# A dense GELU layer, forward and backward, on one core: half products of two step pairs in one run, output units by twos

## The chip, the cores and the metric

The kernel runs on one core of a Trainium2 chip. The time is the device time of one execution in microseconds (us), the median of several runs; less is better. A profiled execution stands beside it: its trace names every instruction of every engine with its start and length.

## What is computed

One layer with a GELU between two matrix products, its output, and the gradients of all five inputs. All tensors are bf16; x and grad_out are 2048 x 448, w1 is 448 x 1792, w2 is 1792 x 448.

```python
def _fwd_reference(x, w1, b1, w2, b2):
    h = jnp.einsum("bsd,df->bsf", x, w1) + b1
    h = _gelu(h)                       # tanh approximation
    return jnp.einsum("bsf,fd->bsd", h, w2) + b2

def reference(x, w1, b1, w2, b2, grad_out):
    ...
    _out, _vjp = jax.vjp(_f, x, w1, b1, w2, b2)
    _grads = _vjp(grad_out)
    return (_out0, *[jnp.asarray(_g) for _g in _grads])
```

In words: u = x w1 + b1, h = gelu(u), out = h w2 + b2; q = grad_out w2', gh = gelu'(u) q, grad_x = gh w1', and the gradients of w1, b1, w2 and b2 from x, gh, h and grad_out.

## The kernel before

The 2048 rows are cut into four blocks of 512, the 1792 hidden columns into fourteen tiles of 128. A step g (0 to 27) is one block with a pair of hidden tiles; there are seven steps in a block. Everything in a step is kept transposed: 128 hidden columns on the partitions, 512 rows along the free axis, two tiles side by side.

A step's work on TensorE:

- **M1** (L242, matmuls at L250) multiplies u's three full slices of 128 of the 448 inner columns, for both tiles: six matmuls of 512 columns.
- **rest** (L253) is what is left of 448: 64 rows. u's half (L260) sits in rows 64 to 127 of the array, q's half (L263) in rows 0 to 63, so that one of each can run beside the other. A call of rest issues u's halves of step g + 1 in turn with q's halves of step g. A pair of such matmuls is called a slot below, and the halves of one call a run.
- **M4** (L266, L269) adds q's three full slices: six matmuls.
- **products** (L432): 448-column matmuls that multiply a finished h or gh tile into out or grad_x. A Unit (L414) is 128 rows of out ("o") or grad_x ("g") and needs fourteen products; 32 units make 448 products.

ScalarE's part (L290): two copies of u out of PSUM with the bias (L294), the square (L295), the GELU (L296), and after VectorE's cubic term the tanh (L390). VectorE's part: the cubic term into B (dve_first, L387), the slope p (L394), two small steps and a product (L395 to L397), and the gate (L401), which reads q from PSUM and writes gh. V, A and B have one buffer each, so that ScalarE's copy for a step waits for VectorE's cubic term of the step before, and its square for p of the step before.

PSUM has eight banks of 512 f32 columns per partition. Before: two for u (one tile), two for q (one tile), four ("acc", L65) that go round for the units. Each unit is evicted by itself (L440): grad_x and the first two units of block 0 by ScalarE (L446), the other out units by VectorE with b2 added (L448). Two units share a staging tile and one store, issued by GpSimd (L452).

The order is written out by hand (manual schedule); each engine works through its own instructions in program order and waits where data or a buffer is not there. The loop (L501) does, per step: rest, M4, evictions, gate, ScalarE's and VectorE's first half for step g + 1, the second half, then products, then M1 of step g + 2. In block 0 the products of its own four out units are run as h comes up (grow, L474): eight a step. From step 7 on there are twelve products a step, in block 3 sixteen. GpSimd's queue also stores h to DRAM (L405), for the turned loads later; SP's queue turns gh into natural order (L410) and loads the next blocks of x and grad_out (L149, L167).

After the steps, GpSimd reloads x and grad_out in natural order over the places of w1 and w2' (L549, L550), eight units of block 3 are left on TensorE, and SP loads h turned (L562). Then come the gradients of w1 (L598, L606) and of w2 (L617), whose results go round the same four banks. VectorE and GpSimd sum the gradients of the biases beside them.

Of the kernel before, what the change touches and what calls it, by code (L numbers as in the profile page):

```python
# [18 lines left out]
def kernel(  # L19
# [44 lines left out]
    psum_u = ctx.enter_context(tc.tile_pool(name="psum_u", bufs=1, space=bass.MemoryType.PSUM))  # L64
    psum_a = ctx.enter_context(tc.tile_pool(name="psum_a", bufs=4, space=bass.MemoryType.PSUM))  # L65

    first = ExitStack()
    psum_h = first.enter_context(tc.tile_pool(name="psum_h", bufs=1, space=bass.MemoryType.PSUM))

# [172 lines left out]
    def M1(g):  # L242
        if g == 0:
            u_of[g] = [psum_a.tile([P, SB], F32, name="acc")[:] for h in range(2)]
        else:
            u = psum_u.tile([P, 2, SB], F32, name="u")
            u_of[g] = [u[:, h, :] for h in range(2)]
        for h in range(2):
            for kt in range(KF):
                nc.tensor.matmul(u_of[g][h], lhsT=w1_sb[:, 1 + kt, cols(g, h)], rhs=xq(g // NPAIR)[:, 1 + kt, :],  # L250
                                 start=(kt == 0), stop=False, skip_group_check=True)

    def rest(gu, gg):  # L253

        if gg is not None:
            q = psum_g.tile([P, 2, SB], F32, name="q")
            g_of[gg] = q
        for h in range(2):
            if gu is not None:
                nc.tensor.matmul(u_of[gu][h], lhsT=w1_sb[DL:P, 0, cols(gu, h)], rhs=xq(gu // NPAIR)[DL:P, 0, :],  # L260
                                 start=False, stop=True, tile_position=(DL, 0), skip_group_check=True)
            if gg is not None:
# [23 lines left out]
    def keep_warm(n, weights, moving):  # L286
        for i in range(n):
            nc.tensor.matmul(pw[:], lhsT=weights, rhs=moving, start=True, stop=True)

    def act_first(g):  # L290
# [4 lines left out]
        nc.scalar.activation(out=A_of(g), in_=V_of(g), func=ACT.Square, scale=math.sqrt(3.0 * GELU_C * GELU_A))  # L295
        nc.scalar.activation(out=hT(g), in_=V_of(g), func=ACT.Gelu_apprx_tanh)  # L296

    def first_products():

        u_of[0] = [[t[:, 0:HB] for t in ua], [psum_h.tile([P, SB], F32, name="h%d" % h)[:, 0:HB] for h in range(2)]]  # L300
# [12 lines left out]
    def turn_w2():  # L313

        for kt in range(KD):
            n = DL if kt == KF else P
            for h in range(2):
                o = (2 * (kt % 2) + h) * P
                nc.tensor.matmul((ta, pw)[kt // 2][0:n, o:o + P], lhsT=w2_sb[:, h, kt * P:kt * P + n], rhs=ident,
                                 start=True, stop=True)  # L320

    def turned(i):
        nc.scalar.copy(out=w2T_sb[:, 2 * i:2 * i + 2, 0:2 * P], in_=(ta, pw)[i].rearrange("p (k f) -> p k f", k=2))

    def first_chain():
# [52 lines left out]
        for r in range(2):  # L378
            first_q(r, (0, 1))
            run_pieces([U["o", 0, r]] * 2)  # L380
# [10 lines left out]


    def dve_second(g):
        nc.vector.scalar_tensor_tensor(out=p_of(g), in0=A_of(g), scalar=GELU_C, in1=hT(g), op0=ALU.add, op1=ALU.mult)  # L394
        nc.vector.tensor_scalar(out=t_of(g), in0=t_of(g), scalar1=1.0, scalar2=None, op0=ALU.add)  # L395
        nc.vector.tensor_scalar(out=p_of(g), in0=p_of(g), scalar1=-0.5, scalar2=None, op0=ALU.add)  # L396
        nc.vector.tensor_tensor(out=t_of(g), in0=t_of(g), in1=p_of(g), op=ALU.mult)  # L397

# [15 lines left out]
    class Unit:  # L414
        def __init__(self, kind, b, j):
            self.kind, self.b, self.j, self.done, self.ps = kind, b, j, 0, None

            self.by_act = kind == "g" or (b == 0 and j < 2)

        def piece(self):  # L420
            ft = self.done
            c, h = divmod(ft, 2)
            g = self.b * NPAIR + c
            if self.ps is None:
                self.ps = psum_a.tile([P, SB], F32, name="acc")
            js = slice(self.j * P, (self.j + 1) * P)
            if self.kind == "o":
                lhsT, rhs = hT(g)[:, h, js], w2_sb[:, ft, :]
            else:
                lhsT, rhs = ghT(g)[:, h, js], w1T_sb[:, ft, :]  # L430
            bias = self.by_act and self.kind == "o"
            nc.tensor.matmul(self.ps[:, 0:D], lhsT=lhsT, rhs=rhs, start=(ft == 0), stop=(ft == NF - 1 and not bias))  # L432
            if bias and ft == NF - 1:
                nc.tensor.matmul(self.ps[:, 0:D], lhsT=w128[:], rhs=b2_bc[:], start=False, stop=True)
            self.done += 1
            return self.done == NF

    stage = {}

    def evict(un):  # L440
        key = (un.kind, un.b, un.j // 2)
        if key not in stage:
            stage[key] = iop.tile([P, 2, D], BF16, name="io_" + un.kind)
        st = stage[key]
        if un.by_act:
            nc.scalar.copy(out=st[:, un.j % 2, :], in_=un.ps[:, 0:D])  # L446
        else:
            nc.vector.tensor_tensor(out=st[:, un.j % 2, :], in0=un.ps[:, 0:D], in1=b2_bc[:], op=ALU.add)  # L448
        dst = out2 if un.kind == "o" else gx2
        if un.j % 2:  # L450
            r0 = row0(un.b) + (un.j - 1) * P
            nc.gpsimd.dma_start(out=dst[r0:r0 + 2 * P, :].rearrange("(j p) d -> p j d", p=P), in_=st[:])  # L452

    full = []

    def run_pieces(units):
        for un in units:
            if un.piece():
                full.append(un)

    def flush(by_act=None):
        for un in [un for un in full if by_act in (None, un.by_act)]:
            full.remove(un)
# [193 lines left out]
```

## Time and profile before

| | us |
|---|---|
| median of 3 runs | 275.22 (275.17 to 275.58) |
| the profiled execution, its own time | 274.79 |
| span of its trace (first to last instruction) | 273.0 |
| TensorE busy in the span | 267.8 |
| VectorE busy | 193.1 |
| ScalarE busy | 145.0 |
| steps of block 0: ended on TensorE at about | 47 |
| gradient of w1 begins (L598) | 184.40 |
| gradient of w2 begins (L617) | 227.3 |

TensorE is called PE in the rows, its weight loads PEld, VectorE DVE, ScalarE ACT, GpSimd POOL and SyncE SP; L432 is line 432 of the kernel. A row names the tile that is written, an arrow and the tiles that are read, and "x12" is twelve instructions. Matmuls overlap: a row's length is that of one matmul from its first to its last work, so the spacing of the starts, and not the lengths, says what TensorE needs. The page's chain is the sequence of work that ended last, followed back from the end; what is not in it had time to spare.

### The profile page before, as it was taken

How to read it: one execution, taken by the hardware profiler on the slowest of the kernel's cores; microseconds unless marked ns; L12 is line 12 of the kernel's file. 1: busy time of each engine (PE TensorE's matmuls, PEld its weight loads, DVE VectorE, ACT ScalarE, POOL GpSimd, SP SyncE). 2: the span in 40 equal slices, each digit the busy share in tenths (PEclk: the TensorE clock that was granted, in tenths of full speed). 3: DMA queues.
4: the chain of work that ended last, by engine and by line, in shares of the span. 5: the costliest groups of instructions: out<-in, count | busy, mean ns of one | idle time of the engine just before them, and what ended most of it. 6: DMA issues, size and time to landing. Idle time of an engine off the chain costs nothing.

```text
span 273.0 us, 3631 instructions
## 1 busy us (share of the span) xinstructions
PE 267.8 (98%) x1411; PEld 124.9 (46%) x1411; DVE 193.1 (71%) x242; ACT 145.0 (53%) x193; POOL 54.2 (20%) x59
## 2 busy tenths in 40 slices
PE   8999999999999999999999999999999999999995
PEld 3434443444444344434444445554445655555552
DVE  6899999999999999999888861139999980000000
ACT  3988879788888788877777740011111221112111
POOL 0000103820401403023022137111700019400000
PEclk9999999999999999999999999999999999999999
DMA  7999899999279928065534239999999951101110
GB/s 172 209 272 227 155 211 187 260 285 242 74 167 223 235 57 170 17 170 131 116 113 87 100 113 223 257 331 251 188 245 259 184 143 58 52 2 50 53 50 34
DMA packets 100477, 43.52 MB, mean 159 GB/s; under 512 B 89036, under 2 KB 97100, under 8 KB 100460
## 3 DMA queue, kind: packets, MB, share of 16 engines
q1 hardware_dynamic: 93376, 26.65, 51.2%
q0 software_dynamic: 4512, 14.69, 17.0%
q10 hardware_dynamic: 2572, 1.95, 2.4%
q8 instruction: 11, 0.18, 0.3%
q14 instruction: 6, 0.05, 0.1%
HBM read 7.00 MB, written 14.23 MB: 78 GB/s over the span
## 4 chain that ended last, share of the span: by engine, by line
PE 84%; DVE 12%; DMA 2%; ACT 0%; issue 0%; DVEq 0%
PE acc L432 27%; PE acc L617 16%; PE acc L598 13%; PE q L269 10%; PE u L250 10%; PE u L260 4%; DVE T L394 3%; DVE Bt L387 3%; DVE ghT_h L401 3%; PE acc L606 2%; DVE T L397 2%; DMA xg_h<-in_x_dram 2%; DVE T L395 1%; PE h L282 1%; DVE T L396 1%; PE acc L305 0%
## 5 line engine op out<-in xcount | busy, mean ns | idle before, releaser
L432 PE MATMUL acc<-w_gw,hT_h 128*128 128x448 bf16 x224 | 46.6, 353 | 0.0
L432 PE MATMUL acc<-w1T_gw,ghT_h 128*128 128x448 bf16 x224 | 45.1, 352 | 0.0
L294 ACT ACTIVATE VA<-u,b_col 128x512 f32<-128x512 f32 x54 | 34.0, 681 | 13.4 <-PE u L260 13.4
L250 PE MATMUL u<-xg_h,w_x 128*128 128x512 bf16 x162 | 39.4, 379 | 0.6 <-ACT VA L294 0.6
L269 PE MATMUL q<-xg_h,w2T_g 128*128 128x512 bf16 x162 | 39.6, 381 | 0.0
L401 DVE SCALAR_TENSOR_TENSOR ghT_h<-T,q 128x1024 bf16<-128x1024 bf16 x27 | 32.9, 1220 | 8.0 <-PE q L269 6.6
L598 PE MATMUL acc<-gh_nat,w_x 128*128 128x512 bf16 (+1 forms) x192 | 36.7, 353 | 0.0
L390 ACT ACTIVATE T<-Bt 128x1024 bf16<-128x1024 f32 x27 | 28.5, 1057 | 13.2 <-DVE Bt L387 13.1
L394 DVE SCALAR_TENSOR_TENSOR T<-VA,hT_h 128x1024 bf16<-128x1024 f32 x27 | 33.1, 1226 | 0.0
L387 DVE SCALAR_TENSOR_TENSOR Bt<-VA 128x1024 f32<-128x1024 f32 x27 | 32.9, 1218 | 0.0
L432 PEld LDWEIGHTS <-hT_h 128*128 128x128 bf16 x224 | 21.8, 98 | 21.2 <-issue 0.2
L432 PEld LDWEIGHTS <-ghT_h 128*128 128x128 bf16 x224 | 21.9, 98 | 20.9
L583 DVE TENSOR_TENSOR VA<-VA,gh_nat 128x1792 f32<-128x1792 f32 x14 | 30.0, 2142 | 0.5
L295 ACT ACTIVATE VA<-VA 128x1024 f32<-128x1024 f32 x27 | 28.5, 1057 | 0.9
L296 ACT ACTIVATE hT_h<-VA 128x1024 bf16<-128x1024 f32 x27 | 28.1, 1040 | 0.0
L598 PEld LDWEIGHTS <-w_x 128*128 128x128 bf16 x192 | 18.7, 98 | 17.7 <-issue 0.4
L269 PEld LDWEIGHTS <-w2T_g 128*128 128x128 bf16 x162 | 13.6, 97 | 24.2 <-issue 11.4
L619 ACT CAST w_gw<-acc 128x448 bf16<-128x448 f32 x13 | 6.9, 533 | 32.6 <-PE acc L617 32.6
L250 PEld LDWEIGHTS <-w_x 128*128 128x128 bf16 x162 | 15.8, 98 | 18.4 <-issue 0.8
L600 ACT CAST w1T_gw<-acc 128x512 bf16<-128x512 f32 (+1 forms) x12 | 6.3, 533 | 30.1 <-PE acc L598 23.0
L446 ACT CAST io_g<-acc 128x448 bf16<-128x448 f32 x16 | 8.3, 520 | 22.6 <-PE acc L432 22.6
L405 POOL DMA_DIRECT2D hT_dram<-hT_h x28 | 20.3, 727 | 0.2 <-issue 0.2
(79 smaller groups left out, 245.4 us busy)
## 6 DMA issues: line engine op xcount, KB each, us to landing
hT_dram<-hT_h POOLq DMA_DIRECT2D x28, 256.0 KB, 4.0
out_dram<-io_o POOLq DMA_DIRECT2D x8, 224.0 KB, 3.8
out_dram<-io_g POOLq DMA_DIRECT2D x8, 224.0 KB, 3.2
w_x<-in_x_dram POOLq DMA_DIRECT2D x1, 1344.0 KB, 11.9
w2T_g<-in_grad_out_dram POOLq DMA_DIRECT2D x1, 1344.0 KB, 15.2
out_dram<-w_gw SPq DMA_DIRECT2D x4, 336.0 KB, 2.4
w_x<-in_w_dram SPq DMA_DIRECT2D x2, 384.0 KB, 4.2
out_dram<-w1T_gw ACTq DMA_DIRECT2D x2, 384.0 KB, 4.0
```

Of the source, the lines that this page charges most:

```text
L250: nc.tensor.matmul(u_of[g][h], lhsT=w1_sb[:, 1 + kt, cols(g, h)], rhs=xq(g // NPAIR)[:, 1 + kt, :], start=(kt == 0), stop=False, skip_grou ...
L269: nc.tensor.matmul(g_of[g][:, h, :], lhsT=w2T_sb[:, kt, cols(g, h)], rhs=gq(g // NPAIR)[:, kt, :], start=False, stop=(kt == KF - 1), skip_ ...
L294: nc.scalar.activation(out=V_of(g)[:, h, :], in_=u[h], func=ACT.Identity, bias=b1_col[:, ft:ft + 1])
L295: nc.scalar.activation(out=A_of(g), in_=V_of(g), func=ACT.Square, scale=math.sqrt(3.0 * GELU_C * GELU_A))
L387: nc.vector.scalar_tensor_tensor(out=B_of(g), in0=A_of(g), scalar=3.0 * GELU_C, in1=V_of(g), op0=ALU.add, op1=ALU.mult)
L390: nc.scalar.activation(out=t_of(g), in_=B_of(g), func=ACT.Tanh, scale=-1.0 / 3.0)
L394: nc.vector.scalar_tensor_tensor(out=p_of(g), in0=A_of(g), scalar=GELU_C, in1=hT(g), op0=ALU.add, op1=ALU.mult)
L401: nc.vector.scalar_tensor_tensor(out=ghT(g), in0=t_of(g), scalar=1.0, in1=q[:], op0=ALU.add, op1=ALU.mult)
L432: nc.tensor.matmul(self.ps[:, 0:D], lhsT=lhsT, rhs=rhs, start=(ft == 0), stop=(ft == NF - 1 and not bias))
L583: nc.vector.tensor_tensor(out=gsb_v, in0=gsb_v, in1=gh_rows(st, 0, NF), op=ALU.add)
L598: nc.tensor.matmul(psv, lhsT=x_all[:, st, kt * P:(kt + 1) * P], rhs=gh_rows(st, a0, a1), start=(st == 0), stop=(st == NS - 1))
L617: nc.tensor.matmul(ps[:, 0:D], lhsT=h_blk[ft][:, st, :], rhs=g_all[:, st, :], start=(st == 0), stop=(st == NS - 1))
```

## The change

PSUM is dealt out anew: four tiles of two banks each, named x, y, z and w. x and y hold u, z and w hold q; the units use them in between. In block 0 the order of the first six steps is as before, with y and w holding the four growing out units.

From step 7 on, the loop goes once for step 7 and then by two steps, a and a + 1. One call of rest issues the halves of u for two steps and of q for two steps: four slots in one run. Then come M4(a) and M4(a + 1), three matmuls of M1, two whole units (28 products) that are run in z, once the gate of step a has read q out of it, and the other nine matmuls of M1. The two units are evicted by one instruction of 2 x 448 elements, before ScalarE's and VectorE's second half for the later step. For the lone step 7 the units go to w. In steps 26 and 27 there is no u left, so q's halves run by themselves.

At the end of block 0, step 7's chain is taken apart: the two evictions of block 0's out units stand between its square and its GELU on ScalarE, and between p and the small steps on VectorE, and M1 of steps 8 and 9 follow at once. out(3, 0) and (3, 1) are run in the double step 24, before the last M4; three pairs of units are left for after the steps. Loads of the next blocks, stores of h and the turning of gh are placed at other steps. The gradients' results go round x, y, w, z, the first bank of each.

The core of the diff, from which lines that only leave are left out in the loop and the unit code (they stand in the kernel above):

```diff
@@ -61,11 +61,16 @@
     const = ctx.enter_context(tc.tile_pool(name="const", bufs=1))
     iop = ctx.enter_context(tc.tile_pool(name="iop", bufs=2))
     dram = ctx.enter_context(tc.tile_pool(name="dram", bufs=1, space=bass.MemoryType.DRAM))
-    psum_u = ctx.enter_context(tc.tile_pool(name="psum_u", bufs=1, space=bass.MemoryType.PSUM))
-    psum_a = ctx.enter_context(tc.tile_pool(name="psum_a", bufs=4, space=bass.MemoryType.PSUM))
-
+
+
+
+    psum_s = ctx.enter_context(tc.tile_pool(name="psum_s", bufs=1, space=bass.MemoryType.PSUM))
     first = ExitStack()
     psum_h = first.enter_context(tc.tile_pool(name="psum_h", bufs=1, space=bass.MemoryType.PSUM))
+
+    def pair(name):
+        return (psum_z if name == "z" else psum_s).tile([P, 2, SB], F32, name=name)
+
 
     hT_dram = dram.tile([F, S], BF16, name="hT_dram")
     hT_dram_v = hT_dram.rearrange("(ft p) s -> p ft s", p=P)
@@ -239,27 +244,25 @@
     u_of = {}
     g_of = {}
 
-    def M1(g):
-        if g == 0:
-            u_of[g] = [psum_a.tile([P, SB], F32, name="acc")[:] for h in range(2)]
-        else:
-            u = psum_u.tile([P, 2, SB], F32, name="u")
-            u_of[g] = [u[:, h, :] for h in range(2)]
-        for h in range(2):
+    def M1(g, u, hs=(0, 1)):
+        u_of[g] = [u[:, h, :] for h in range(2)]
+        for h in hs:
             for kt in range(KF):
                 nc.tensor.matmul(u_of[g][h], lhsT=w1_sb[:, 1 + kt, cols(g, h)], rhs=xq(g // NPAIR)[:, 1 + kt, :],
                                  start=(kt == 0), stop=False, skip_group_check=True)
 
-    def rest(gu, gg):
-
-        if gg is not None:
-            q = psum_g.tile([P, 2, SB], F32, name="q")
+    def rest(us, qs):
+
+        for gg, q in qs:
             g_of[gg] = q
-        for h in range(2):
-            if gu is not None:
+        for i in range(2 * max(len(us), len(qs))):
+            n, h = divmod(i, 2)
+            if n < len(us):
+                gu = us[n]
                 nc.tensor.matmul(u_of[gu][h], lhsT=w1_sb[DL:P, 0, cols(gu, h)], rhs=xq(gu // NPAIR)[DL:P, 0, :],
                                  start=False, stop=True, tile_position=(DL, 0), skip_group_check=True)
-            if gg is not None:
+            if n < len(qs):
+                gg, q = qs[n]
                 nc.tensor.matmul(q[:, h, :], lhsT=w2T_sb[0:DL, KF, cols(gg, h)], rhs=gq(gg // NPAIR)[0:DL, KF, :],
                                  start=True, stop=False, tile_position=(0, 0), skip_group_check=True)
 
...
-    def act_first(g):
+            nc.tensor.matmul(tp[:, 1, :], lhsT=weights, rhs=moving, start=True, stop=True)
+
+    def act_copy(g):
         u = u_of.pop(g)
         for h in range(2):
             ft = 2 * (g % NPAIR) + h
             nc.scalar.activation(out=V_of(g)[:, h, :], in_=u[h], func=ACT.Identity, bias=b1_col[:, ft:ft + 1])
         nc.scalar.activation(out=A_of(g), in_=V_of(g), func=ACT.Square, scale=math.sqrt(3.0 * GELU_C * GELU_A))
+
+    def act_gelu(g):
         nc.scalar.activation(out=hT(g), in_=V_of(g), func=ACT.Gelu_apprx_tanh)
 
+    def act_first(g):
+        act_copy(g)
+        act_gelu(g)
+
...
-    def dve_second(g):
+    def dve_p(g):
         nc.vector.scalar_tensor_tensor(out=p_of(g), in0=A_of(g), scalar=GELU_C, in1=hT(g), op0=ALU.add, op1=ALU.mult)
+
+
+    def dve_rest(g):
         nc.vector.tensor_scalar(out=t_of(g), in0=t_of(g), scalar1=1.0, scalar2=None, op0=ALU.add)
         nc.vector.tensor_scalar(out=p_of(g), in0=p_of(g), scalar1=-0.5, scalar2=None, op0=ALU.add)
         nc.vector.tensor_tensor(out=t_of(g), in0=t_of(g), in1=p_of(g), op=ALU.mult)
+
+    def dve_second(g):
+        dve_p(g)
+        dve_rest(g)
 
...
-    class Unit:
-        def __init__(self, kind, b, j):
-            self.kind, self.b, self.j, self.done, self.ps = kind, b, j, 0, None
-
-            self.by_act = kind == "g" or (b == 0 and j < 2)
...
+    def product(out, kind, b, j, ft, bias=False):
+        c, h = divmod(ft, 2)
+        g = b * NPAIR + c
+        js = slice(j * P, (j + 1) * P)
+        if kind == "o":
+            lhsT, rhs = hT(g)[:, h, js], w2_sb[:, ft, :]
         else:
+            lhsT, rhs = ghT(g)[:, h, js], w1T_sb[:, ft, :]
+        nc.tensor.matmul(out, lhsT=lhsT, rhs=rhs, start=(ft == 0), stop=(ft == NF - 1 and not bias))
+
+    def send(kind, b, j, st):
+        r0 = row0(b) + j * P
+        dst = out2 if kind == "o" else gx2
+        nc.gpsimd.dma_start(out=dst[r0:r0 + 2 * P, :].rearrange("(j p) d -> p j d", p=P), in_=st[:])
+
+
+    grown = {}
+
+    def grow(g, js):
+        for j in js:
+            if g == 0 and j % 2 == 0:
+                grown[j] = pair("yw"[j // 2])
+            for h in range(2):
+                product(grown[j - j % 2][:, j % 2, 0:D], "o", 0, j, 2 * g + h, j < 2)
+
+
+    def run_two(kind, b, j, t, f0=0, f1=NF):
+        for i in range(2):
+            for ft in range(f0, f1):
+                product(t[:, i, 0:D], kind, b, j + i, ft)
+        return kind, b, j, t
+
+    def evict_two(kind, b, j, t, by_act=False):
+        st = iop.tile([P, 2, D], BF16, name="io_" + kind)
+        if kind == "g" or by_act:
+            nc.scalar.copy(out=st[:], in_=t[:, :, 0:D])
+        else:
+            nc.vector.tensor_tensor(out=st[:], in0=t[:, :, 0:D], in1=b2_bc[:, None, :].to_broadcast([P, 2, D]), op=ALU.add)
+        send(kind, b, j, st)
+
...
+    M1(1, pair("x"))
+    rest([1], [])
     first_chain()
     first.close()
+    psum_z = ctx.enter_context(tc.tile_pool(name="psum_z", bufs=1, space=bass.MemoryType.PSUM))
+
+    for g in range(NPAIR):
         if g > 0:
+            rest([g + 1], [(g, pair("z"))])
             M4(g)
             dve_gate(g)
+        if g < NPAIR - 1:
+            act_first(g + 1)
+            dve_first(g + 1)
+            act_second(g + 1)
+            dve_second(g + 1)
+            grow(g, range(2 if g == 0 else 0, SPB))
+            M1(g + 2, pair("x"))
+            continue
+
+        grow(g, range(2))
+        for j in range(2):
+            nc.tensor.matmul(grown[0][:, j, 0:D], lhsT=w128[:], rhs=b2_bc[:], start=False, stop=True)
+        grow(g, range(2, SPB))
+        act_copy(g + 1)
+        evict_two("o", 0, 0, grown[0], True)
+        act_gelu(g + 1)
+        dve_first(g + 1)
+        act_second(g + 1)
+        dve_p(g + 1)
+        evict_two("o", 0, 2, grown[2])
+        dve_rest(g + 1)
+    M1(NPAIR + 1, pair("x"))
+    M1(NPAIR + 2, pair("y"))
+
+
+
+    TWOS = {7: ("g", 0, 0), 8: ("g", 0, 2), 10: ("o", 1, 0), 12: ("o", 1, 2), 14: ("g", 1, 0), 16: ("g", 1, 2),
+            18: ("o", 2, 0), 20: ("o", 2, 2), 22: ("g", 2, 0), 24: ("g", 2, 2)}
+    TURNS = {8: [(0, 0, 2)], 10: [(0, 2, 4)], 12: [(0, 4, 7)], 14: [(1, 0, 2)], 16: [(1, 2, 4)], 18: [(1, 4, 7)],
+             20: [(2, 0, 2)], 22: [(2, 2, 4), (2, 4, 7)], 24: [(3, 0, 2)], 26: [(3, 2, 4), (3, 4, 7)]}
+    for a, n in [(NPAIR, 1)] + [(g, 2) for g in range(NPAIR + 1, NSTEP, 2)]:
+        nxt = [g for g in (a + n, a + n + 1) if g < NSTEP]
+        rest(nxt, [(a + i, pair("zw"[i])) for i in range(n)])
+        for i in range(n):
+            M4(a + i)
+        dve_gate(a)
+        if nxt:
+            act_first(nxt[0])
+            dve_first(nxt[0])
+
+        f1 = NF - 2 if a == NPAIR + 3 else NF
+        m = [g for g in (a + n + 2, a + n + 3) if g < NSTEP]
+        if m:
+            mx = pair("x")
+            if n == 2:
+                M1(m[0], mx, [0])
+        two = run_two(*TWOS[a], pair("w" if n == 1 else "z"), 0, f1) if a in TWOS else None
+        if nxt:
+            act_second(nxt[0])
+            dve_second(nxt[0])
+        if n == 2:
+            dve_gate(a + 1)
+        if nxt:
+            act_first(nxt[1])
+            dve_first(nxt[1])
+        if m:
+            M1(m[0], mx, range(n - 1, 2))
+        if f1 < NF:
+            run_two(*two, f1, NF)
+        if m:
+            M1(m[1], pair("y"))
+        if two is not None:
+            evict_two(*two)
+        if nxt:
+            act_second(nxt[1])
+            dve_second(nxt[1])
+        if a + n + 2 == NSTEP:
+            evict_two(*run_two("o", NB - 1, 0, pair("x")))
+        if a in (NPAIR, 12):
+            load_x(2 if a == NPAIR else 3)
+            load_g(2 if a == NPAIR else 3)
+        for t in TURNS.get(a, []):
             turn_gh(*t)
+        store_some(2 * n, a + n)
+    store_some(NSTEP, NSTEP)
...
+    for kind, j, name in (("o", 2, "y"), ("g", 0, "x"), ("g", 2, "z")):
+        evict_two(*run_two(kind, NB - 1, j, pair(name)))
...
+    turn = 0
+
+    def bank():
+        nonlocal turn
+        turn += 1
+        return pair("xywz"[turn % 4])[:, 0, :]
```

## The prediction

> **What bounds the kernel now.** I read the page's first two parts, then TensorE's waits, then the chain that ended last, then timelines. The page:
>
> ```profile
> span 273.0 us, 3631 instructions
> PE 267.8 (98%) x1411; PEld 124.9 (46%) x1411; DVE 193.1 (71%) x242; ACT 145.0 (53%) x193; POOL 54.2 (20%) x59
> PEclk9999999999999999999999999999999999999999
> ```
>
> TensorE is busy at full clock throughout, and its waits sum to 2.0 us, of which 0.6 lies inside the kernel: M1 of step 9 (L250) waited for ScalarE's copy (L294), until 47.63. Before 47.6 the chain runs over VectorE (5.07 us a step in block 0), after it over TensorE alone. So what counts after 47.6 is TensorE's own time, and whether a wait gets into it. The chain over one step, start and length:
>
> ```profile
> 60.31 1.29 PE u L250 x6
> 61.61 0.32 PE u L260
> 61.93 0.00 PE q L263
> 61.93 0.21 PE u L260
> 62.14 0.00 PE q L263
> 62.15 1.40 PE q L269 x6
> 63.55 2.27 PE acc L432 x12
> 65.81 0.22 PE u L250
> ```
>
> A step is 65.81 - 60.31 = 5.50 us. Six M1 matmuls take 1.29 (0.2155 each), twelve products 2.27 (0.189), but six M4 matmuls take 1.40 and the two slots of half products 0.53. Starts on TensorE show why:
>
> ```profile
> 61.23 0.38 PE L250 MATMUL u<-xg_h,w_x 128*128 128x512 bf16 x1
> 61.54 0.39 PE L260 MATMUL u<-xg_h,w_x 64*128 64x512 bf16 x1
> 61.54 0.39 PE L263 MATMUL q<-xg_h,w2T_g 64*128 64x512 bf16 x1
> 61.77 0.38 PE L260 MATMUL u<-xg_h,w_x 64*128 64x512 bf16 x1
> 61.77 0.38 PE L263 MATMUL q<-xg_h,w2T_g 64*128 64x512 bf16 x1
> 62.08 0.39 PE L269 MATMUL q<-xg_h,w2T_g 128*128 128x512 bf16 x1
> ```
>
> A u and a q half start together and share a slot. The next slot follows after 0.23, but going into halves and coming out costs 0.31 each, not 0.2155: about 0.2 us for each run of halves, whatever its length.
>
> **What is removed: ten runs of halves.** One run costs a step less its full matmuls: 5.505 - 12 x 0.189 - 12 x 0.2155 = 0.65 us with two slots (starts alone give 0.31 + 0.23 + 0.31 - 0.2155 = 0.63). A run of four slots is not in the trace; I take 0.65 + 2 x 0.23 = 1.11 (by 0.2155 a slot 1.08; by 0.31, as if each slot paid the entry, 1.27). After step 7 the kernel before has 20 runs of two (g = 8 to 27), 13.0 us. The changed one has ten of four (a = 8 to 26; the last holds q's halves alone, unpaired), 11.1 us. Gain **1.9 us**, bounds 0.3 to 2.2. All 448 products and all full matmuls remain; they only move.
>
> **The transition out of block 0.** Times are those of before, carried on. Up to product 42.90 nothing differs. M1(8) runs 42.90 to 44.19. M1(9) now follows at once, in tile y, and needs ScalarE's eviction of the first output pair: square(7) ends 43.6, the eviction (two of 448 in a row took 0.95) ends 44.45, so TensorE waits **0.3**. M1(9) ends 45.79, the run of four 46.90, M4(7) 48.19. Here products of block 1 begin; before they began at 48.92, with the same work done and four products (0.76) more. VectorE meanwhile: gelu(7) now comes behind the eviction, so p(7) starts at 45.5, not 45.25; the output eviction (1.07) now lies before t + 1; gate(7) starts at 49.4, not 48.93. That lateness comes back once: gate(7) 49.4, first(8) 50.5, p(8) 51.6, copy(9) 52.7 to 54.0, square(9) to 55.05, first(9) 55.1, gelu(9) to 56.0, and only then the ScalarE eviction of tile w, to 56.85. TensorE's next run wants w in its third slot at 56.62: **0.3** wait. gate(8) ends 60.7, and the products that reuse its tile z come at 60.67: **0.1**.
>
> **A double step in steady state**, from the first half at 0: four slots; M4(a) 1.0 to 2.3, its result at 2.45; M4(a+1) to 3.6; three M1 to 4.25; 28 products in z to 9.5; nine M1 to 11.5. Period 28 x 0.189 + 24 x 0.2155 + 1.11 = 11.58. Each wait that this adds:
> - Products into z wait for gate(a) (1.22): 2.5 to 3.7, against 4.25. Hidden by M4(a+1) and three M1, 0.5 over. Everything on TensorE is queued behind it.
> - q into z waits for the eviction. On ScalarE (gx) it runs 9.7 to 10.65, on VectorE (out) 9.8 to 10.9, against 11.58. Hidden by nine M1, 0.7 over; for a = 10, whose last four products come late, 0.1 over.
> - The eviction delays tanh(n1) on ScalarE or p(n1) on VectorE, behind which t + 1, -0.5, the product and gate(a') of the next double stand. Rows (p to t + 1 1.21, 0.34, 0.46, 0.79) put gate(a') at 13.3 or 13.6, against its q at 14.0.
> - M1 into x and y waits for ScalarE's copies, over 1 us earlier.
>
> An eviction of 2 x 448 is not in the trace. The nearest row is two back to back:
>
> ```profile
> 84.37 0.69 DVE L397 TENSOR_TENSOR T<-T 128x1024 bf16<-128x1024 bf16 x1
> 84.98 1.15 DVE L448 TENSOR_TENSOR io_o<-acc,b_bc 128x448 bf16<-128x448 f32 x2
> 86.05 1.21 DVE L401 SCALAR_TENSOR_TENSOR ghT_h<-T,q 128x1024 bf16<-128x1024 bf16 x1
> ```
>
> 1.07 from start to the next start; bounds 0.62 (one of 448) and 1.24 (two apart). The saved overhead itself is worth nothing, because VectorE and ScalarE are not in the chain here.
>
> **The end.** At a = 24 no M1 remains to hide gate(24): products wait from 3.6 to 3.75, **0.2** with its release. out(3, 0) now runs before the last M4, so three pairs of units (84 products, 15.9 us) follow M4(27) instead of 16 + 112 products (24.2 us). Under these x and g are reloaded. The GpSimd queue is the place to look: send of out(3, 0), then four stores of h (0.73 each), then x at 168.2 instead of 164.97; it landed 11.9 and 12.1 us after issue before, so 180.1 and 181.4, and L598 wants the first at about 183.1 and the second 2.6 later. 3 us over, less what 1 MB of stores just ahead takes (some 2 us). The turning of gh for steps 25 to 27 goes out at 168.4 and is wanted at 193; h's turned blocks ended at 219 and are wanted from 227. Nothing. SP's loads for block 2 and 3 move earlier and are wanted earlier, ten us later at least.
>
> **Sum.** Products from 48.92 to L598's start at 184.40 took 135.48 before. After: 48.19 + 135.48 + 0.76 - 1.9 = 182.53, with waits of 0.3 (w), 0.1 (gate 8) and 0.2 (a = 24) 183.1 (the 0.3 at y lies already in 48.19). That is 1.3 us earlier, and L598 onwards is unchanged work. Own time of the profiled execution 274.79 (span 273.0, 1.8 around it) becomes 273.5; on the median of 275.22, 0.43 above it, **273.9**.
>
> **Rivals.**
> 1. Longer runs hide no load (chance 0.12): slots three and four pay 0.31, ten runs of 1.27; the gain of 1.9 becomes 0.3, the waits of 0.6 turn it: 275.2 + 0.3 = 275.5. Against it: the second slot already follows by 0.23 and its weight loads start at 61.55. The Trainium skill has a rule of this kind (TensorE: Matmul & The Clock Gate, Part 3, "What overlaps and what doesn't"): a weight load overlaps running matmuls only when its row group differs. By that rule the two added slots of a run would each show a load of 0.09; the trace speaks against it, since full matmuls on all rows follow each other by 0.2155 with loads of 0.098 between.
> 2. The gate comes late, the slower side (0.16). The loop: products end 5.45 after they start, eviction 1.07, p 1.21, 0.34, 0.46, 0.79, gate 1.22: 10.6 from one start of products to the earliest next, against 11.58 on TensorE (11.3 for a = 10). If eviction and handovers cost over 1 us more than these rows, VectorE sets the period; it decides from 11.8, where nine doubles lose 2. At 11.95, 3.3 lost: 277.2. For it: VectorE is 96 to 98% busy in this stretch. Against it: the two margins above.
> 3. x lands late (0.07): the wait at L598 takes the gain. If it took 15.4 us, as g did, 0.5 is lost: 274.4; slower than before only from 17 us on.
> 0.05 is left for orders that the trace of before doesn't suggest.
>
> The forecast has 0.60. Within 0.2% (0.55 us, about what a measurement of this kernel can tell from no change) lies most of rival 1 and a little of 2: 0.14. Faster: the forecast, rival 3 mostly: 0.64. Slower: 0.22. Range: no waits and slots of 0.2155 give 272.9 below; above, rival 1 and half of rival 2: 276.4.
>
> **What would show it.** Eleven runs of halves after 45 us, slots 0.23 apart inside a run (rival 1: 0.31). A period of 11.6 from a = 10 to 24. TensorE's waits: about 0.3 for ScalarE near 44.5 and 56.9, 0.1 to 0.2 for gate(24), none else (rival 2: waits for L401's successor in each double). L598 starting near 183.1 without a wait for DMA (rival 3). The forecast is wrong if the start of L598 is not 1 to 2 us earlier, or if anything behind it grows.

## The result and the profile after

| | us |
|---|---|
| median of 6 runs | 290.98 (289.15 to 295.52), forecast 273.9 |
| ratio to the kernel before | 1.0546 (95%: 1.0517 to 1.0576) |
| the profiled execution, its own time | 290.93 (before 274.79) |
| span | 289.2 (before 273.0) |
| the last product starts on TensorE | 183.42 (before 184.21) |
| gradient of w1 begins (now L627) | 197.58 (before 184.40) |
| gradient of w2 begins (now L646) | 243.34 (before 227.21) |

The ratios here and below leave out the executions that ran in a slower state, which are two of these six.

The kernel became 5.5% slower, and all of it lies behind the products. Lines of the changed kernel: M1 is L251, the halves L262 and L266, M4 L272, products L437, ScalarE's evictions L464, VectorE's L466, the turning of gh L425, stores of h L420, the reload of x and g L574 and L575.

The page's first two parts of the kernel after:

```profile
span 289.2 us, 3582 instructions
PE 267.6 (93%) x1397; PEld 127.2 (44%) x1411; DVE 193.5 (67%) x235; ACT 143.2 (50%) x184; POOL 54.5 (19%) x59
PEclk9999999999999999999999999956999999999999
```

The engines' busy times are within 2% of those of before; only the span grew, by 16.2. The clock has a dip, in slices 27 and 28 of 40 (188 to 202 us). So look for a wait just ahead. TensorE's waits after (line and tile, what it waited for, sum, times, longest):

```profile
PE y L627 <- DMA w_x<-in_x_dram: 13.8, 1, 13.8
PE x L627 <- ACT w1T_gw L629: 1.5, 1, 1.5
```

The first is x in natural order, reloaded over the place of w1. The chain of work that ended last, at that place:

```profile
169.27 28.26 DMA w_x<-in_x_dram
...
197.58 4.99 PE y L627 x16
202.57 3.45 PE w L627 x16
```

x landed 28.26 us after its issue; before it took 11.9. The sixteen matmuls behind the wait took 4.99 and the next sixteen 3.45: 1.54 lost to the lower clock. What else went out just then stands on two queues. Timelines of SP and of GpSimd after (start, length of the issue, engine, line):

```profile
169.17 16.42 SPq L425 DMA_TRANSPOSE gh_nat<-ghT_h  x1
```

```profile
166.37 2.90 POOL L420 DMA_DIRECT2D hT_dram<-hT_h  x4
169.27 1.05 POOL L574 DMA_DIRECT2D w_x<-in_x_dram  x1
```

and SP's of before:

```profile
161.74 5.20 SPq L410 DMA_TRANSPOSE gh_nat<-ghT_h  x1
```

The turning of gh for steps 25 to 27 now goes out 0.10 us ahead of x, right behind four stores of h; before it went out 3.2 us ahead (161.74 against 164.97). Its issue took 16.42 instead of 5.20, and it landed after 30.2 instead of 13.1.

The second wait is a consequence. ScalarE's timeline after, in the gradient of w1:

```profile
209.51 0.59 ACT L629 CAST w1T_gw<-z 128x512 bf16<-128x512 f32 x1 [2.87 <-PE z L627]
223.81 0.43 ACTq L630 DMA_DIRECT2D out_dram<-w1T_gw  x1
224.29 0.59 ACT L629 CAST w1T_gw<-x 128x512 bf16<-128x512 f32 x1 [14.19 <-DMA hT_h<-hT_dram]
```

ScalarE's store (L630) stood until a turned load of h on SP's queue had landed, and the next copy out of PSUM stood behind it, 14.19 idle in all. Before, this idle time was 7.04 and cost nothing:

```profile
202.58 1.07 ACT L600 CAST w1T_gw<-acc 128x512 bf16<-128x512 f32 x2 [7.04 <-DMA hT_h<-hT_dram]
```

The account of 290.93 - 274.79 = 16.14: the last product starts 0.79 earlier. From there to the first matmul of L627 it takes 14.16 instead of 0.19, so 13.97 more (the wait for x of 13.8, and the overlap of two neighbouring matmuls). The lower clock adds 1.54, the second wait 1.5: together 16.2.

### The profile page after: what moved, and what is told of

Same layout as the page of the kernel before. It is cut to its first block, busy times and chain, and to the rows that moved or that the text cites. A ratio compares the mean times of both kernels' runs of the same rounds, so it can differ in the third digit from the quotient of the medians.

```text
span 289.2 us, 3582 instructions
## 1 busy us (share of the span) xinstructions
PE 267.6 (93%) x1397; PEld 127.2 (44%) x1411; DVE 193.5 (67%) x235; ACT 143.2 (50%) x184; POOL 54.5 (19%) x59
## 4 chain that ended last, share of the span: by engine, by line
PE 61%; DVE 13%; DMA 13%; ACT 5%; SPq 3%; issue 2%; POOL 1%; ACTq 0%; DVEq 0%
PE z L437 17%; DMA w_x<-in_x_dram 10%; PE z L646 4%; PE x L646 4%; PE z L272 4%; PE y L251 4%; PE w L272 4%; PE y L627 4%; PE x L251 3%; PE w L646 3%; PE y L646 3%; DVE ghT_h L416 3%; DVE T L402 3%; DVE Bt L396 3%; SPq L584 3%; PE z L627 2%
## 5 line engine op out<-in xcount | busy, mean ns | idle before, releaser
L627 PEld LDWEIGHTS <-w_x 128*128 128x128 bf16 x192 | 19.0, 100 | 34.3 <-DMA w_x<-in_x_dram 14.2
L437 PE MATMUL z<-w1T_gw,ghT_h 128*128 128x448 bf16 x168 | 32.8, 352 | 0.1
L437 PEld LDWEIGHTS <-ghT_h 128*128 128x128 bf16 x224 | 21.9, 98 | 21.2 <-issue 0.7
L437 PEld LDWEIGHTS <-hT_h 128*128 128x128 bf16 x224 | 21.8, 98 | 20.8 <-issue 0.2
L627 PE MATMUL y<-gh_nat,w_x 128*128 128x512 bf16 (+1 forms) x64 | 14.1, 378 | 13.8 <-DMA w_x<-in_x_dram 13.8
L297 ACT ACTIVATE VA<-x,b_col 128x512 f32<-128x512 f32 x34 | 21.4, 681 | 8.6 <-PE x L262 8.5
L272 PE MATMUL z<-xg_h,w2T_g 128*128 128x512 bf16 x101 | 24.7, 381 | 0.2 <-issue 0.2
L416 DVE SCALAR_TENSOR_TENSOR ghT_h<-T,z 128x1024 bf16<-128x1024 bf16 x17 | 20.7, 1220 | 6.0 <-PE z L272 5.3
L251 PE MATMUL x<-xg_h,w_x 128*128 128x512 bf16 x89 | 23.8, 379 | 0.7
L272 PEld LDWEIGHTS <-w2T_g 128*128 128x128 bf16 x162 | 14.5, 98 | 22.3 <-issue 7.2
L251 PEld LDWEIGHTS <-w_x 128*128 128x128 bf16 x162 | 15.8, 98 | 18.5 <-issue 0.4
L437 PE MATMUL z<-w_gw,hT_h 128*128 128x448 bf16 x112 | 22.0, 352 | 0.0
L420 POOL DMA_DIRECT2D hT_dram<-hT_h x28 | 20.3, 727 | 0.0
L408 DVE TENSOR_TENSOR T<-T 128x1024 bf16<-128x1024 bf16 x27 | 18.7, 692 | 0.9
L442 POOL DMA_DIRECT2D out_dram<-io_o x8 | 6.0, 751 | 58.3 <-DVE io_o L466 43.8
## 6 DMA issues: line engine op xcount, KB each, us to landing
w_x<-in_x_dram POOLq DMA_DIRECT2D x1, 1344.0 KB, 28.3
```

Source lines behind the costliest of these rows:

```text
L272: nc.tensor.matmul(g_of[g][:, h, :], lhsT=w2T_sb[:, kt, cols(g, h)], rhs=gq(g // NPAIR)[:, kt, :], start=False, stop=(kt == KF - 1), skip_ ...
L416: nc.vector.scalar_tensor_tensor(out=ghT(g), in0=t_of(g), scalar=1.0, in1=q[:], op0=ALU.add, op1=ALU.mult)
L437: nc.tensor.matmul(out, lhsT=lhsT, rhs=rhs, start=(ft == 0), stop=(ft == NF - 1 and not bias))
L627: nc.tensor.matmul(psv, lhsT=x_all[:, st, kt * P:(kt + 1) * P], rhs=gh_rows(st, a0, a1), start=(st == 0), stop=(st == NS - 1))
```

## The experiments

Two theories at first. **Collision**: the turning and the reload slow each other when they go out at the same moment. **Order**: x is late only because it goes out later, behind four stores and a send. Edits are to the changed kernel unless another is named. Landing is counted from issue.

**e1, x early.** x is reloaded behind the last halves, at 151.63; g stays.

```diff
+        if a == NSTEP - 4:
+            reload(x_all, x2)
...
-    for dst, src in ((x_all, x2), (g_all, g2)):
+    reload(g_all, g2)
```

> The changed kernel with one edit: GpSimd's queue reloads x at double step 24, right behind the last half products of u, instead of behind the stores of h after the steps. Theory (the turning of gh for steps 25 to 27, issued at 169.17, and the reload, issued at 169.27, are in flight together and slow each other, so x lands after 28.3 us instead of 11.9): x lands long before the turning, TensorE doesn't wait at L627, and the 13.8 us of wait, the 1.5 us that the lower clock behind it cost and the 1.5 us of the later wait for ScalarE's copy all go: 291.0 - 16.8 = 274.2. If the lost time lay in TensorE's own work or in the order of the steps: still over 285.

285.68, ratio 1.0296 (1.0212 to 1.0380); the four executions spread from 281.59 to 288.79, and the profiled one took 288.79. x landed after 7.8, long before its use, and yet most of the loss stayed: now g's reload (169.65) met the turning (169.55) behind the same stores, g took 28.7 and the turning 31.5, and TensorE waited 4.0 for the turned gh and 6.2 for ScalarE's copy. The forecast missed, but Order falls: it isn't x, but whichever reload goes out with the turning.

**e2, the turning later.** The last turning goes behind four turned loads of h.

```diff
-             20: [(2, 0, 2)], 22: [(2, 2, 4), (2, 4, 7)], 24: [(3, 0, 2)], 26: [(3, 2, 4), (3, 4, 7)]}
+             20: [(2, 0, 2)], 22: [(2, 2, 4), (2, 4, 7)], 24: [(3, 0, 2)], 26: [(3, 2, 4)]}
...
+        if ft == 3:
+            turn_gh(3, 4, 7)
```

> The changed kernel with the turning of gh for steps 25 to 27 issued behind the first four turned loads of h on SP's queue; the reload stays where it is. Theory (this turning and the reload slow each other): x lands 12 to 14 us after its issue, no wait at L627, 274 to 276. Rival (the 1 MB of h that is stored just ahead on the same queue holds x back): x still takes 28 us, 291. Rival (any transposing transfer beside the reload does it): the first turned load of h starts near 173 and takes the turning's place, x takes over 20 us, 282 or more.

273.91, ratio 0.9945 (0.9925 to 0.9965): the whole loss is gone, with the four stores and the order of the GpSimd queue as they were. TensorE has no wait left but one of 1.2 at the start. Timelines of SP and GpSimd of e2:

```profile
172.15 16.40 SPq L425 DMA_TRANSPOSE gh_nat<-ghT_h  x1
```

```profile
169.10 1.05 POOL L574 DMA_DIRECT2D w_x<-in_x_dram  x1
```

x is 3.05 us ahead and landed after 11.9, as before the change. The edit also moves SP's first turned loads of h forward, and the fourth of them went out 1.35 ahead of x:

```profile
167.75 4.30 SPq L584 DMA_TRANSPOSE xg_h<-hT_dram  x1
```

It landed after 11.7. So a transposing transfer beside the reload is not enough for the collapse. Inside the transfers the difference is plain. DMA from 178 to 184 us, after and then e2 (queue, packets, MB, share of the 16 engines' time; q1 carries SP's transposing transfers, in after the turning alone, q0 those of GpSimd, the reload above all):

```profile
DMA packets 819, 0.97 MB, mean 162 GB/s; under 512 B 626, under 2 KB 642, under 8 KB 819
...
q1 hardware_dynamic: 610, 0.16, 86.9%
q0 software_dynamic: 209, 0.81, 36.1%
```

```profile
DMA packets 1042, 2.24 MB, mean 373 GB/s; under 512 B 548, under 2 KB 580, under 8 KB 1042
...
q0 software_dynamic: 526, 2.11, 94.6%
q1 hardware_dynamic: 516, 0.12, 10.1%
```

In both, both queues are at work. In e2 a packet of q1 takes 0.101 x 16 x 6 us / 516 = 19 ns, after 137 ns; a packet of the reload takes 0.17 us in both, but 209 get through instead of 526. So it isn't more bytes: the turning's small packets became seven times as long, and fewer of the reload's get through beside them. Which of the two brings about the other is not shown.

**e3, stores behind the reload.**

```diff
-        store_some(2 * n, a + n)
-    store_some(NSTEP, NSTEP)
+        if a < NSTEP - 4:
+            store_some(2 * n, a + n)
...
+    store_some(NSTEP, NSTEP)
```

> The changed kernel with the four stores of h of double steps 24 and 26 behind the reload on GpSimd's queue, so that x is issued near 166.4, 2.8 us ahead of the turning of gh. Theory (turning and reload slow each other while both are in flight): x takes over 20 us all the same, a wait of 4 to 11 us stays, 279 to 288. Rival (the stores ahead hold x back): 12 us, no wait, 274. Rival (who is issued first gets through): also about 12 us, 274.

275.05, ratio 0.9984 (0.9971 to 0.9998). x went out 2.8 ahead of the turning and landed after 8.2. That mends the collapse, but it moves the moment as well as the stores, so it doesn't tell them apart. (These times are of the profiled execution, which took 278.69, 3.6 over the median.)

**e4, the kernel before, made to meet.** The last send goes behind the reload, so that x goes out 0.01 behind the turning, with two stores of h ahead.

```diff
-    flush()
...
+    flush()
```

> The kernel before with its last send of grad_x ahead of the reload moved behind it, so that x is issued near 161.8 instead of 164.97, at the same time as the turning of gh for steps 25 to 27 (161.74). Theory (turning and reload in flight together): though issued 3.2 us earlier, x lands some 28 us later, near 190, TensorE waits about 5 us before L598, 280 to 283, and the turning takes about 30 us instead of 5. Rival (only the changed kernel's four stores hold x back): x lands after 12 us, 275.2, no change.

275.69, ratio 1.0022 (1.0002 to 1.0043): the forecast missed. x took 17.6 (11.9 before) and the turning 18.1 (13.1 before): slower, but no collapse, and x's cover hid nearly all of it. The same moment alone isn't enough.

**e5, x early and g late.** e1, with g reloaded behind the send of the first grad_x pair after the steps, near 180. Stores and turning stay together.

```diff
-    reload(g_all, g2)
...
+        if name == "x":
+            reload(g_all, g2)
```

> The changed kernel with x reloaded at double step 24 (as in the first experiment) and grad_out reloaded only behind the send of the first pair of grad_x units of block 3, near 180. The turning of gh for steps 25 to 27 stays where the change has it, so it meets the four stores of h but no reload. Theory (the collapse needs a reload beside the turning): the turning lands 5 to 8 us after its issue, TensorE never waits behind 184, 273.4 to 274.0. Rival (the turning and the four stores of h are enough): the turning takes 20 us or more, TensorE waits for it near 194, over 278.

273.79, ratio 0.9944 (0.9930 to 0.9959). Here four stores and the turning go out together without a reload, and the turning landed after 7.6. So the collapse takes the reload too.

**e7, e9, e10: the moment.** A copy of one element of the last gh on GpSimd holds the reload until the gate is done (e7 on e3, without stores ahead; e9 on the changed kernel, with all four). e10 holds the turning back instead, by multiplications of gh by 1.0.

```diff
+    nc.gpsimd.tensor_copy(out=w128[:, 0:1], in_=ghT(NSTEP - 1)[:, 0, 0:1])
```

```diff
+        for _ in range(3 if a + n == NSTEP else 0):
+            nc.vector.tensor_scalar(out=ghT(NSTEP - 1), in0=ghT(NSTEP - 1), scalar1=1.0, scalar2=None, op0=ALU.mult)
```

> The third experiment (the four stores of h behind the reload) with one more edit: GpSimd copies one element of gh of step 27 ahead of the reload, so that the reload goes out just behind the turning instead of 2.8 us ahead of it. Theory (who is issued first decides, and a turning that starts at the reload's side slows both): x lands after 20 us or more, TensorE waits, 280 to 292. Rival (the four stores just ahead of the reload are needed for the collapse): x lands after 8 to 14 us, or the turning first and x 5 us behind it (17.6 us in the fourth experiment): 274 to 277.

> The changed kernel with one small copy on GpSimd that waits for gh of step 27 ahead of the reload: the four stores of h stay just ahead of it, but the reload goes out about 0.8 us behind the turning instead of 0.1 us. Theory A (the four stores keep the transfer engines full up to the reload, so the turning never gets them alone): collapse as in the changed kernel, x lands after 20 us or more, 284 to 295. Theory B (only the lag of 0.1 us matters): as in the seventh experiment the turning goes first, x lands after 10 to 14 us, 274 to 278.

> The changed kernel with three multiplications of gh of step 27 by 1.0 on VectorE (0.35 us each) ahead of its turning: the turning is issued about 0.9 us behind the reload instead of 0.1 us ahead of it. Theory A (stores, reload and turning overlapping do it, whoever is first by so little): x lands after 20 us or more, 284 to 295. Theory B (whoever is first gets through): x lands after 9 to 13 us and the turning after some 20 us, 274 to 276.

e7 took 277.61, ratio 1.0085 (1.0056 to 1.0114). The turning went out 0.79 ahead of x; x landed after 9.7 and the turning after 9.9. That is no collapse; 2.1 are lost elsewhere, in a wait for ScalarE's copy (the turned loads of h come later). e9 took 275.81, ratio 0.9998 (0.9976 to 1.0019): the turning 1.15 ahead, x after 10.8, the turning after 11.2. e10 took 275.61, ratio 1.0009 (0.9994 to 1.0024): the turning 2.08 behind, x after 9.3, the turning after 18.1. e9 and e10 have all four stores right ahead and no collapse: a microsecond or two apart is enough. Both still stand 1.7 to 1.9 over e2, and 1.4 (e9) and 1.5 (e10) of that is TensorE's wait for ScalarE's copy.

**e12, the same moment without the stores.** The four stores go ahead of the send of out(3, 0), and four GpSimd copies in dead buffers stand in their place.

```diff
+            store_some(NSTEP, NSTEP)
...
+    for _ in range(4):
+        nc.gpsimd.tensor_copy(out=VA_flat[:, 2 * SB:3 * SB], in_=VA_flat[:, 3 * SB:4 * SB])
```

> The changed kernel with the four stores of h of double steps 24 and 26 ahead of the send of out(3, 0), near 161, and four copies on GpSimd (about 0.65 us each, within a tile that is read no more) in their old place, so that the reload still goes out near 169.3, close to the turning, with no store just ahead. Theory (stores and the same moment of issue are both needed): no collapse, the turning or the reload goes first, x lands after 8 to 18 us, 273.5 to 277. Rival (the same moment of issue is enough): turning and reload take over 25 us, 284 to 295.

283.02, ratio 1.0279 (1.0203 to 1.0354): under the rival's 284 and far over the theory's 277. The turning went out 0.06 behind x; x took 15.7, g 18.7. The issue of the turning fell to 4.15 and it landed after 20.5. Half the loss stayed, by another way: the first turned load of h took 16.48 to issue, ScalarE's copy stood 18.4, and TensorE waited 5.8 for it and 1.1 for x. The stores are part of the collapse, not all of it.

**e13, e14: the kernel before, with stores and moment.** e4, with the stores of steps 24 and 25 held back (four ahead), and the turning delayed by four (e13) or two (e14) multiplications of gh by 1.0.

```diff
-            if g >= NPAIR - 1 and stored < g:
+            if g >= NPAIR - 1 and stored < g and stored < NSTEP - 4:
...
+        for _ in range(2 if g == NSTEP - 1 else 0):
+            nc.vector.tensor_scalar(out=ghT(g), in0=ghT(g), scalar1=1.0, scalar2=None, op0=ALU.mult)
```

> The fourth experiment (the kernel before with its last send of grad_x behind the reload) with the stores of h of steps 24 and 25 held back to those of 26 and 27, so that four stand just ahead of the reload and it goes out near 163.4, and with four multiplications of gh of step 27 by 1.0 on VectorE ahead of its turning, so that it goes out near 163.4 too. Theory (four stores and the same moment of issue): the kernel before collapses as well, turning and reload take over 25 us, x lands near 189 or later, TensorE waits 4 us or more before or inside L598, 280 to 293. Rival (something else of the changed kernel is needed): as in the fourth experiment, 275 to 277.

> The thirteenth experiment with two multiplications instead of four, each of which took 0.7 us there: in the kernel before, four stores of h, then the reload near 163.8, and the turning of steps 25 to 27 near 163.7. Theory (four stores just ahead and the same moment of issue): the kernel before collapses too, turning and reload take over 25 us, x lands near 189, 280 to 293. Rival (something else of the changed kernel is needed, or the window of moments is narrower than 0.2 us): x lands after 11 to 18 us, 275 to 277.

e13 took 275.23, ratio 1.0000 (0.9988 to 1.0011). It missed the moment: the turning went out 1.33 behind x, and x landed after 11.2. e14 took 292.17, ratio 1.0606 (1.0573 to 1.0640): the turning 0.45 ahead, x after 31.7, g after 34.9, the turning after 40.6. SP's turning and GpSimd's reload of x, then TensorE's waits in e14:

```profile
163.53 22.36 SPq L410 DMA_TRANSPOSE gh_nat<-ghT_h  x1
163.98 1.05 POOL L550 DMA_DIRECT2D w_x<-in_x_dram  x1
```

```profile
PE acc L600 <- DMA w_x<-in_x_dram: 10.4, 1, 10.4
PE acc L600 <- ACT w1T_gw L602: 2.0, 1, 2.0
```

These are the two waits of the changed kernel, in a kernel with none of its runs of four slots, tiles or units by twos. The collapse belongs to the meeting, not to the edit's substance.

The runs by the turning's issue less the reload's, one profiled execution each (e6 and e8 have e2's order and its landings within 1.1):

| run | turning less reload | stores of h right ahead | reload landed | turning landed |
|---|---|---|---|---|
| before | -3.23 | 0 | 11.9 | 13.1 |
| e9 | -1.15 | 4 | 10.8 | 11.2 |
| e7 | -0.79 | 0 | 9.7 | 9.9 |
| e14 | -0.45 | 4 | 31.7 | 40.6 |
| after | -0.10 | 4 | 28.3 | 30.2 |
| e1 (g) | -0.10 | 4 | 28.7 | 31.5 |
| e4 | -0.01 | 2 | 17.6 | 18.1 |
| e12 | +0.06 | 0 | 15.7 | 20.5 |
| e13 | +1.33 | 4 | 11.2 | 21.5 |
| e10 | +2.08 | 4 | 9.3 | 18.1 |
| e3 | +2.80 | 0 | 8.2 | 20.7 |
| e2 | +3.05 | 4 | 11.9 | 19.8 |

With four stores ahead, the reload took 28.3 to 31.7 where the turning went out 0.10 to 0.45 ahead of it, and no more than 12.0 where the turning was 1.15 ahead, or 1.33 and more behind. With two stores or none, at nearly the same moment, it took 15.7 to 17.6. With four stores no run lies between 0.45 and 1.15 ahead, or between 0.10 ahead and 1.33 behind, so the edges of the window are known only so far. Why both stay slow for some 28 us once they have started together was not found.

**e8, the price of a run.** e2 with each run of four cut into two, each ahead of its M4.

```diff
-        rest(nxt, [(a + i, pair("zw"[i])) for i in range(n)])
-        for i in range(n):
-            M4(a + i)
+        qs = [(a + i, pair("zw"[i])) for i in range(n)]
+        if n == 1:
+            rest(nxt, qs)
+            M4(a)
+        else:
+            for i in range(n):
+                rest(nxt[i:i + 1], qs[i:i + 1])
+                M4(a + i)
```

> The kernel of the second experiment with the run of four slots cut in two again: half products of u(n0) and q(a), M4(a), half products of u(n1) and q(a + 1), M4(a + 1), everything else as it was. By the prediction's price for a run (0.65 us with two slots, 1.11 with four), ten doubles pay 0.19 more each: 273.9 + 1.9 = 275.8. If the saving lay elsewhere (fewer evictions, the order of the steps): 273.9.

275.64, ratio 1.0009 (0.9992 to 1.0025): 1.73 over e2, for ten runs more; the forecast had 1.9.

**e6 and e11, the start.** Block 0 began late (below). u of step 0 in two tiles, one for each half of the rows: e6 on e2, e11 on e5.

```diff
-    ua, tp = pair("y"), pair("w")
+    ua, tp = (pair("y"), pair("x")), pair("w")
```

> The kernel of the second experiment (turning behind the first four turned loads of h) with the first u of step 0 in two tiles, half 0 in y and half 1 in x, where the change has both halves in y. Theory (VectorE's first copy out of y waited for ScalarE's first copy out of the same tile, 7.12 against 6.12 before; 0.5 us of that is the wait, the rest a later start of the matmuls): VectorE's first copy starts together with ScalarE's, block 0 begins 0.5 us earlier, 273.9 - 0.5 = 273.4. Rival (block 0 is set by something else): 273.9.

> The fifth experiment (x reloaded at double step 24, grad_out near 180) together with the first u of step 0 in two tiles (sixth experiment). The two gains against the changed kernel are in different places: 273.8 less 0.2: 273.6. If the one takes the other's cover: 273.8 or more.

e6: 273.69, ratio 0.9938 (0.9922 to 0.9955). VectorE's first copy starts at 6.20, not 6.94, but M1 of step 1 now waits 0.44 for that copy to leave tile x, and M1 of step 8 is only 0.16 earlier: of the 0.5 expected, 0.2 came. e11: 274.35, ratio 0.9961 (0.9931 to 0.9991): no better than e5 or e6. e2, e5 and e6 are all some 0.6% faster than the kernel before, and their differences lie inside the intervals.

## Why the prediction was wrong, step by step

**Right: the runs.** The chain of the kernel after, over one double step:

```profile
101.68 0.59 PE x L251 x2
...
103.57 0.32 PE x L262
...
103.89 0.21 PE x L262
...
104.11 0.21 PE y L262
...
104.33 0.21 PE y L262
...
104.54 1.40 PE z L272 x6
...
107.88 5.30 PE z L437 x28
113.18 0.05 issue
113.23 0.59 PE x L251 x2
```

The period is 113.23 - 101.68 = 11.55 (forecast 11.58). Inside a run, slots three and four follow by 0.21, so rival 1 (0.31) falls; e8 gives the price of a run again. The rule of the Trainium skill that rival 1 was set beside (TensorE: Matmul & The Clock Gate, Part 3, "What overlaps and what doesn't") doesn't hold here: the added slots follow without a gap for their weight loads of 0.09.

**Right: gates and evictions.** 2 x 448 took 0.91 on ScalarE and 1.09 on VectorE (forecast 1.07), M1 of step 9 waited 0.30 for ScalarE's eviction (0.3), and at a = 24 the 28 products took 5.46, not 5.30 (0.2). q's third slot in the first run, the wait for w, came 0.06 behind u's (57.49 and 57.43; forecast 0.3). Rival 2 falls: between products and M1 no more than 0.05 a double step is left ("issue" above).

**Missed, small: the start.** The prediction had no difference up to 42.90. In fact block 0 began late: gate(1) at 18.41, before 17.50. VectorE's timelines, before and then after, at its first copy of u:

```profile
6.12 0.48 DVE L332 TENSOR_SCALAR VA<-acc,b_col 128x256 f32<-128x256 f32 x1 [1.18 <-PE acc L308]
```

```profile
7.12 0.48 DVE L341 TENSOR_SCALAR VA<-y,b_col 128x256 f32<-128x256 f32 x1 [1.85 <-ACT VA L340]
```

Before, the two banks of u for step 0 were two tiles; now they are one tile y, and VectorE's copy of one bank waits for ScalarE's copy of the other. TensorE also began 0.18 later (4.93 and 5.11, waiting for x in both). M1 of step 8, which the forecast carried over at 42.90, started at 43.81: 0.91 late. So the products ended 0.79 earlier than before and not 1.3. Some 0.4 of the 0.9 came back: the wait for w took 0.06 instead of 0.3, and eight double steps took 11.55 instead of 11.58. Two tiles alone (e6) bring back only 0.2, and how the other 0.7 are made up was not taken apart further.

**The step that failed: the end.** The prediction read the GpSimd queue in its new order rightly ("x at 168.2 instead of 164.97"; it was 169.27), but carried the old landing time over: "it landed 11.9 and 12.1 us after issue before, so 180.1 and 181.4". And for the turning, which by its own figure would go out at 168.4: "Nothing." The two issue times, 0.2 us apart, stand a few lines from each other and were never put together. Each transfer was priced as if alone; in the trace of before they were 3.2 apart. With e2's order, where they are 3.05 apart the other way, x takes 11.9 again, the gradient of w1 begins at 183.45 (forecast 183.1) and the time is 273.91, against 273.9 forecast. Its profiled execution took 273.88, against 273.5 forecast for one; the medians agree better only because this one doesn't stand 0.43 above its profiled execution.

Rival 3 named the wait (x late, "slower than before only from 17 us on"), not the meeting behind it, and took 15.4 as its price, from the slowest reload in the trace; 28.3 was outside all of its rows. The range had no room for it.

Two rules of the Trainium skill bear on it (DMA: Bandwidth & Descriptors). "Rules for kernel authors" says "A transpose next to ordinary DMAs needs nothing"; it is said of keeping the data right, and for the time it misleads here: 28.3 us against 11.9. "Queues, rings and completion order" says that each transfer engine takes turns between its queues, a whole packet of several descriptors from each. The trace of after counts 610 of the turning and 209 of the reload, that of e2 516 and 526; whether what it counts is such a packet no run here shows, so the rule is neither borne out nor refuted.

**Also missed: what stands behind.** "L598 onwards is unchanged work" is true of TensorE, but the turned loads of h wait in SP's queue behind the slow turning (next issue at 185.82), and ScalarE's store and copies wait for them. This second way cost 1.5 in the changed kernel, 6.2 in e1 and 5.8 in e12, where TensorE waited 1.1 at most for x itself. The lower clock behind the long wait, 1.54, was not in the sum either: the granted clock was 0.50 from 190 to 200 us and 0.97 from 200 to 206, and 1.54 lost at half clock stands, by estimate, for 3.1 us of work. The Trainium skill (TensorE: Matmul & The Clock Gate, Part 1, "What's actually happening") has an idle array fall to half clock and stay there for some 3.4 us of new work; the trace agrees.

## What to carry to other kernels

When an edit moves transfers, write down the issue times of all large ones on all queues side by side; where two that were apart come within half a microsecond, as here, the old landing times are no price, and the range needs an end far above them. A gain of 0.6% on the busiest engine was real here, and an edit that moved one transfer by three microseconds decided between it and a loss of 5.5%. When the span grows while all busy times stand still, go straight to the waits and from there to the queues, not to the part of the edit that was meant to matter.

## What was not expected of the hardware

A turning of gh (SBUF to SBUF, on SP's queue) and a reload of 1344 KB (GpSimd's queue), issued together behind four stores, moved 162 GB/s in after and 124 in e14 from 178 to 184 us, against 373 in e2 with the same two under way 3 us apart. Issued within half a microsecond of each other they moved less than half as much, and landed after 28 to 41 us. And ahead of the reload by 0.79 or 1.15, the turning was done after 9.9 and 11.2, sooner than with any order in which it came behind (18.1 to 21.5).
